# Seven places for gate/up weights in the first quarter of a GEGLU feed-forward, and one low-half computation moved from GpSimd to VectorE

## The chip, the cores and the metric

The kernel runs on one core of a Trainium2 chip. The metric is the device time of one execution in microseconds; three executions are timed and the median counts. One execution is also recorded by the hardware profiler. TensorE does the matmuls, VectorE and ScalarE the elementwise work and the moves out of PSUM, GpSimd some elementwise work on SBUF, and SyncE issues every transfer (DMA) from one queue, in program order.

## The reference

One transformer block with Fourier mixing and a gated feed-forward, for 2048 tokens of 448 features, hidden size 1792, all in float32:

```python
def _A_ref(x, dft_seq_re, dft_seq_im, dft_hid_re, dft_hid_im):
    a = jnp.einsum("bsd,ed->bse", x, dft_hid_re)
    b = jnp.einsum("bsd,ed->bse", x, dft_hid_im)
    return jnp.einsum("ts,bse->bte", dft_seq_re, a) - jnp.einsum("ts,bse->bte", dft_seq_im, b)

def _B_ref(x, w_gate, w_up, w_down):
    g = jnp.einsum("bsd,df->bsf", x, w_gate)
    u = jnp.einsum("bsd,df->bsf", x, w_up)
    return jnp.einsum("bsf,fd->bsd", _gelu(g) * u, w_down)

h = x + _A_ref(_layernorm(x), ...)
h2 = h + _B_ref(_layernorm(h), ...)
```

## The kernel before

**Number format.** Every float32 factor of a matmul is split into two float16 parts, a high half (`hi_part`, line 99, on ScalarE) and a low half (`lo_part`, line 102, on VectorE: the scaled source minus the high half). A product is three matmuls: high by high, high by low, low by high. Sums of blocks (Strassen's scheme) save some of the block products.

**Feature stage.** The tokens form sixteen tiles of 128. Each tile is normalised (`x_stats`, `x_root`, `x_rstd`, `x_norm`), split (`x_high`, `x_lo`), turned so that features lie on the partitions, and multiplied by the feature matrix (`feature_mm`), which gives `a` and `b` side by side. The feature matrix comes in four row blocks k = 0 to 3, block 3 with 64 rows. It is loaded as float32 into `wh_raw` and split into `wh_hi` (`wh_high`) and `wh_lo` (`wh_low`, line 393). `wh_low(k, E)` runs on the engine `E`: on VectorE as one instruction with two SBUF inputs (line 397), on GpSimd as a scaling in place (line 399) and a subtraction (line 400). The work on the first tiles (0, 1, 2, 3, then `a` = 10 and `b` = 11) is written out by hand in lines 705 to 771; each engine runs its share in that order. There, tiles 0 to 3 are turned by TensorE (`x_turn_pe`, PSUM tile `xT_ps`, copied out by ScalarE at line 375). `wh_low(0)`, `(1)` and `(2)` are on VectorE and `wh_low(3, G)` on GpSimd. `feature_mm(i, range(8, 11))` is the part that multiplies by the low halves of blocks 1, 2 and 3; `feature_mm(0, range(8, 11))` follows the turning of tile 3.

**Sequence stage.** From there a planner (`plan`, `todo`) places the work by slots: the remaining tiles, then eight passes over the sequence matrices (`seq_mm`, line 508), eight units each, with VectorE and ScalarE splitting the sequence matrix as it arrives. Meanwhile the gate and up weights are loaded, summed and split (class `Weights`) for each of 14 blocks f of 128 hidden columns. Each block is a float16 tile of 28 x 128 columns and is stored to DRAM (`w_dram[f]`). The order is 13 down to 2, then 0 and 1, so tiles 0, 1 and 2 are still in SBUF when the feed-forward begins; they are `gw[0]`, `gw[1]` and `gw[2]`.

**Feed-forward.** Four quarters q of 512 tokens, 14 blocks f each, are run as 56 iterations t = 14 q + f (the loop at line 1177). In the first quarter an iteration does 39 matmuls of 256 columns (line 913, in `product`) into PSUM banks X, Y and Z. The order on TensorE is:

```python
cur.x_close()
nxt.x_open()
...
cur.y_mid()
nxt.z_open()
nxt.y_open()
cur.y_close()
cur.z_close()
```

`cur` is iteration t, `nxt` is t + 1: the weights of the next iteration are first read in `nxt.x_open()`, early in the present one. `x_open` has ScalarE copy bank X to bank Y (line 952), into which `y_open` goes on adding.

The weight tiles lie in three places in turn: `w_tile` (line 159) takes two from the pool `ring` and one from `ring3`. `gw_load(t)` (line 994) takes the next place and loads `w_dram[t % 14]` into it. Line 1184 calls `gw_load(t + 2)` at the head of iteration t, for t = 1 to 53. The place is that of tile t - 1, so the load may start when the matmuls of iteration t - 1 are done.

Beside this, in the first quarter, the down weights are prepared: `down_prep` loads (`down_load`, line 188, SyncE), sums (`down_sums`, line 192, GpSimd, lines 195 to 198) and splits them (ScalarE and VectorE) over two iterations each. The load for block n + 2 is issued in iteration 2n + 2 behind that iteration's gate/up load; its sums run at the end of iteration 2n + 4.

**Between the stages.** SyncE's queue holds, in this order, the last store of h (`h_store`, line 792), a load of down weights (`down_load(1)`, line 793), then the transfers of the loop. The pool `fpool` of the feed-forward is opened where the sequence stage's pools (`dft`, `p2`) were. Its tag `hh` has two slots, each as large as the hidden state of one quarter (7 x 4 x 256 float32 values for each partition, 28,672 bytes). The quarters 0, 1 and 2 take them in turn (`hh0`, `hh1`, `hh2`), and `h_last` (line 1051) takes one for the last quarter.

Of the kernel before, what the change touches and what calls it, by code (L numbers as in the profile page):

```python
# [8 lines left out]
F16 = mybir.dt.float16  # L9
F32 = mybir.dt.float32  # L10
# [3 lines left out]
P = 128  # L14
S, D, DF = 2048, 448, 1792
NT = S // P
NF = DF // P
# [15 lines left out]
def kernel(  # L33
# [38 lines left out]
    V, A, G, PE = nc.vector, nc.scalar, nc.gpsimd, nc.tensor  # L72
# [3 lines left out]
    small = ctx.enter_context(tc.tile_pool(name="small", bufs=3))  # L76
    ring = ctx.enter_context(tc.tile_pool(name="ring", bufs=2))
# [24 lines left out]
    def lo_part(dst, src, hi, scale=1.0):  # L102
        if isinstance(scale, float) and scale == 1.0:
            V.tensor_sub(dst, src, hi)  # L104
        else:
            V.scalar_tensor_tensor(dst, src, scale, hi, op0=ALU.mult, op1=ALU.subtract)  # L106
# [52 lines left out]
    def w_tile(name, pool):  # L159
        return pool.tile([P, 28 * P], F16, tag="w", bufs=2 if pool is ring else 1, name=name)  # L160
# [6 lines left out]
    def hops_tile(q):  # L167
        hops[q] = ring.tile([P, N_OPS, 2 * P], F16, tag="ops", bufs=2, name=f"hops{q}")
# [12 lines left out]
    def ffn_rstd(q, j):  # L181
        mv, sd = moments[q, j]
        moments[q, j] = mv, rstd(mv, sd, f"h{q}_{j}", const)
# [4 lines left out]
    def down_load(n):  # L188
        wd32[n] = fops.tile([P, 4, HD], F32, tag="tt" if n % 2 else "xn", name=f"wd32_{n}")
        nc.sync.dma_start(wd32[n].rearrange("p (k c) d -> p k (c d)", k=2), w_down[n])  # L190
# [17 lines left out]
    def ffn_norm_act(q, j, h):  # L208

        tag = f"h{q}_{j}"  # L210
        mv, r = moments.pop((q, j))
        xn = fops.tile([P, 2, D], F32, tag="xn", name=f"xn_{tag}")
        nb = small.tile([P, 2], F32, tag="nb", name=f"nb_{tag}")
        V.scalar_tensor_tensor(nb, mv[:, :, 0], -1.0, r, op0=ALU.mult, op1=ALU.mult)
        for g in range(2):
            A.activation(xn[:, g, :], h[:, g, :], AF.Identity, scale=r[:, g : g + 1], bias=nb[:, g : g + 1])
        ffn[q, j] = xn
# [89 lines left out]
    def x_stats(*tiles):  # L307
        n, tag = len(tiles), f"x{tiles[0]}"
        mv = small.tile([P, n, 2], F32, tag=f"mv{n}", name=f"mv_{tag}")
        for g, i in enumerate(tiles):  # L310
            st = small.tile([P, 6], F32, tag="st", name=f"st_x{i}")
            V.bn_stats(st, xt[i][0])
            V.bn_aggr(mv[:, g, :], st)
        norm_x[tiles] = mv
# [4 lines left out]
    def x_rstd(*tiles):  # L319
        mv, sd = norm_x.pop(tiles)  # L320
        r = rstd(mv, sd, f"x{tiles[0]}")
        for g, i in enumerate(tiles):
            norm_x[i] = mv, r, g

    def x_bias(*tiles):
        mv, r, _ = norm_x[tiles[0]]
        nb = small.tile([P, 2], F32, tag="nb", name=f"nb_x{tiles[0]}")
        V.scalar_tensor_tensor(nb, mv[:, :, 0], -1.0, r, op0=ALU.mult, op1=ALU.mult)
        for i in tiles:
            norm_x[i] += (nb,)  # L330

    def x_norm(i):
        x_norm_v(i)
        x_high(i)

    def x_norm_v(i):
        mv, r, g, *nb = norm_x.pop(i)
        xn = xt[i][0]
        if nb:
            A.activation(xn, xn, AF.Identity, scale=r[:, g : g + 1], bias=nb[0][:, g : g + 1])  # L340
        else:
            normed(xn, xn, mv, r, g)
        u, g = divmod(i, 2)
        if g == 0:
            pool = (fops, p1)[ORDER.index(u) % 2]
            t = pool.tile([P, 2, 2 * D], F16, tag="xs", name=f"xs{u}")
            for k in range(2):
                xs[i + k] = t[:, k, :]

    def x_high(i):  # L350
        hi_part(xs[i][:, 0:D], xt[i][0])

    def x_lo(i):
        xn, t = xt[i][0], xs[i]
        lo_part(t[:, D : D + DR], xn[:, DM:D], t[:, DM:D])
        lo_part(t[:, D + DR : 2 * D], xn[:, 0:DM], t[:, 0:DM])
# [12 lines left out]
    def x_turn_pe(i, k0, k1):  # L369
        if k0 == 0:  # L370
            xT_tile(i)
        t = ps_dft.tile([P, 8, P], F16, tag="A", name=f"xT_ps{i}_{k0}")
        for k in range(k0, k1):
            PE.transpose(t[:, k, :], xs[i][:, k * P : (k + 1) * P], ident)
        A.activation(xT[i][:, k0:k1, :], t[:, k0:k1, :], AF.Copy)
# [17 lines left out]
    def wh_low(k, E=V):  # L393
        n = P if k < 3 else DR
        src, hi = wh_raw[k // 2][:n, k % 2, :], wh_hi[:n, k, :]
        if E is V:
            lo_part(wh_lo[:n, k, :], src, hi, D_SC)
        else:
            E.tensor_scalar(src, src, D_SC, None, op0=ALU.mult)
            E.tensor_sub(wh_lo[:n, k, :], src, hi)  # L400
# [218 lines left out]
    def at(t, n, *what):  # L619
        t.setdefault(n, []).extend(what)  # L620
# [112 lines left out]
    feature_mm(0, range(4, 6))  # L733
    x_turn_pe(1, 0, 4)
    x_turn_pe(1, 4, 7)
    wh_low(3, G)
    x_stats(2)
    x_root(2)
    feature_mm(0, range(6, 8))
# [10 lines left out]
    wh_low(2)  # L750
    x_rstd(3)
    x_norm(3)
    x_lo(3)
    a, b = tiles_of[2]
    feature_mm(2, range(7), "A")
# [16 lines left out]
    ring3 = None  # L772
    for n in range(min(todo), len(slots)):
        for _, what in sorted(todo.pop(n, ()), key=lambda t: t[0]):
            what()
        if n == p1_end:
            first.close()
            ring3 = ctx.enter_context(tc.tile_pool(name="ring3", bufs=1))
# [15 lines left out]
    gw = {f: gu[f].w for f in range(3)}  # L794
# [69 lines left out]
    fpool = ctx.enter_context(tc.tile_pool(name="fpool", bufs=1, side="right", reuse_waits="tile"))  # L864
# [63 lines left out]
    hh, hq = {}, {}  # L928

    class GateUp:  # L930
# [58 lines left out]
        def c_last(self):  # L989
            A.activation(self.c12, self.c12, AF.Gelu_apprx_tanh, scale=1.0 / H_SC)  # L990
            c22 = self.hidden(1)
            G.tensor_mul(c22, c22, self.c12)  # L992

    def gw_load(t):
        gw[t] = w_tile(f"gw{t}", ring if t % 3 < 2 else ring3)
        nc.sync.dma_start(gw[t], w_dram[t % NF])


# [36 lines left out]
    def hr_load(p):  # L1035
        hr[p] = pair_tile(f"hr{p}")
        nc.sync.dma_start(hr[p], h_dram[p])
# [12 lines left out]
    def last_begin():  # L1050
        last["h"] = fpool.tile([P, 2, NF, 2 * TQ], F16, tag="hh", bufs=2, name="h_last")
        w = ring.tile([P, N_OPS, 2 * P], F16, tag="ops", bufs=2, name="w_last")
        w = w.rearrange("p o d -> p (o d)")[:, : 4 * NC * HD]
        last["w"] = w.rearrange("p (l n k d) -> p l n k d", l=2, n=NC, k=2)
# [39 lines left out]
    def dn_ahead(t):  # L1094

        if t in (NF - 4, NF - 3):
            dn_sums(t - NF + 4)
        if t == NF - 2:
            dn_split(0)
        if NF <= t < 6 * NC + 12:  # L1100
            dn_sums(t - 12)

    N_GU = 4 * NF
# [4 lines left out]
    def do(t, k):  # L1108
        for what in side.pop((t, k), ()):
            what()  # L1110
# [25 lines left out]
    for t in range(3 * NF, N_GU):  # L1136
        f = t % NF
# [29 lines left out]
    at(side, (25, 4), lambda: ffn_root(NB - 1, 1))  # L1167
    at(side, (27, 1), lambda: ffn_rstd(NB - 1, 1))

    cur = GateUp(0)  # L1170
    cur.x_open()
    cur.z_open()
# [4 lines left out]
    for t in range(N_GU):  # L1177
        q, f = divmod(t, NF)
        if f == 0 and q < 3:
            hh[q] = fpool.tile([P, NC, 4, TQ], F32, tag="hh", bufs=2, name=f"hh{q}")  # L1180
            if 1 <= q <= 2:
                hops_tile(q + 1)
        if 0 < t < N_GU - 2:
            gw_load(t + 2)
        if t == 3 * NF:
            last_begin()
            down_load(0)
            down_load(1)
        if q == 3:
            hq[t] = fpool.tile([P, 2, TQ], F32, tag="hq", bufs=2, name=f"hq{t}")  # L1190
        d = t - NF
        if d >= 0 and d % NC == 1:
            hr_load(d // NC)
        if t in (N_GU - 2, N_GU - 1):
            hr_load(t - N_GU + 8)
        nxt = GateUp(t + 1) if t + 1 < N_GU else None
        if q == 0:
            cur.x_close()
            nxt.x_open()
            if prev:  # L1200
                prev.c_last()
# [5 lines that stand above are left out]
            dn_ahead(t)  # L1207
            if t > 0:
                down_prep(t - 1)
        else:  # L1210
            do(t, 0)
            prev.c_last()
            cur.x_close()
            if t > NF:
                cur.z_open()
            if d + 1 < 6 * NC:
                dn_split(d + 1)
            dn_mm(d, range(0, 8))
            cur.y_mid()
            dn_ahead(t)  # L1220
            dn_mm(d, range(8, 18))
            if nxt:
                nxt.x_open()
            do(t, 1)
            do(t, 4)
            cur.y_close()
            cur.z_close()
            dn_mm(d, range(18, 21))
            do(t, 5)
            if nxt:  # L1230
                nxt.y_open()
            if t == 2 * NC:
                down_hi(NC - 1, 1)
            if t == 2 * NC + 1:
                down_lo(NC - 1, 1)
            do(t, 2)
            do(t, 3)
        prev, cur = cur, nxt
# [72 lines left out]
```

## Time and profile before

| | us |
|---|---|
| median of three runs | 728.72 (728.53 to 728.88) |
| the profiled execution | 728.71 |
| its span, first to last instruction | 726.9 |
| TensorE, matmuls busy | 712.0 (98%) |
| TensorE, weight loads busy | 561.6 (77%) |
| VectorE busy | 510.6 (70%) |
| ScalarE busy | 365.0 (50%) |
| GpSimd busy | 207.9 (29%) |

The transfers moved 142.90 MB, 197 GB/s over the whole span. The mean granted clock of TensorE was 0.998 of full speed. The first gate/up matmul of the feed-forward began at 362.49 us of the span, and the first quarter lasted to about 430 us.

How to read it: "busy" adds up the recorded durations of an engine's instructions. Matmuls overlap in TensorE's pipeline, so a record is longer than the step from one matmul to the next. In a list of waits, each row gives who waited, for whom, the sum in us, how often, and the longest. In a timeline, each row gives start and length in us, engine, line, operation, written tile and read tiles, shapes, count, and in brackets the idle time before it with what ended it.

### The profile page before, as it was taken

To read this page: it belongs to the slowest core of one execution; us is meant where nothing else is said; L and a number is where in the kernel's file an instruction comes from. 1 tells how busy PE (TensorE), PEld (TensorE's weight loads), DVE (VectorE), ACT (ScalarE), POOL (GpSimd) and SP (SyncE) were. 2 spreads that over 40 slices of the span, in tenths; PEclk is the share of its full clock that TensorE was granted. 3 is DMA by queue.
4 is the path that set the end of the run, shared out by engine and by line. 5 is a ranking of instruction groups with operands and counts; after the bars stand their busy time and mean duration, and the time that the engine had idled before them with its cause. 6 is when DMAs were issued, how large, how long until landed. Compare 5 with 4: busy or idle time off the path is not lost.

```text
span 726.9 us, 14535 instructions
## 1 busy us (share of the span) xinstructions
PE 712.0 (98%) x5800; PEld 561.6 (77%) x5800; DVE 510.6 (70%) x1043; ACT 365.0 (50%) x748; POOL 207.9 (29%) x237
## 2 busy tenths in 40 slices
PE   7999999999999999999999999999999999999998
PEld 5556566666767666676788789999999999999998
DVE  6678859998989888989345567576665756667520
ACT  5476644645555545444155555456555545555510
POOL 3023030000000000020014464465563756657230
PEclk9999999999999999999999999999999999999999
DMA  8274444897969699685067754757458486555401
GB/s 326 60 187 93 73 171 148 287 256 259 276 240 282 234 275 326 242 298 187 1 223 240 243 191 169 198 179 223 163 171 205 162 215 223 204 200 203 153 15 64
DMA packets 72340, 142.90 MB, mean 197 GB/s; under 512 B 41296, under 2 KB 47568, under 8 KB 72272
## 3 DMA queue, kind: packets, MB, share of 16 engines
q1 hardware_dynamic: 72272, 141.97, 61.1%
q8 instruction: 45, 0.74, 0.4%
q14 instruction: 23, 0.19, 0.1%
HBM read 112.46 MB, written 20.19 MB: 182 GB/s over the span
## 4 chain that ended last, share of the span: by engine, by line
PE 79%; DVE 10%; DMA 5%; ACT 3%; issue 1%; SPq 0%; DVEq 0%; ACTq 0%
PE acc L508 28%; PE pY L913 13%; PE acc_d L855 11%; PE pZ L913 8%; PE pX L913 8%; PE ab L412 7%; DMA gw<-w_dram 3%; DVE ws L106 2%; DVE xs L104 1%; DMA wr<-in_w_seq_dram 1%; PE last_Z L1079 1%; PE last_X L1079 1%; PE last_Y L1079 1%; DMA gu_raw<-in_w_gu_dram 1%; DVE gu_w L106 1%
## 5 line engine op out<-in xcount | busy, mean ns | idle before, releaser
L508 PE MATMUL acc<-b,ws 128*128 128x448 f16 (+1 forms) x1968 | 280.0, 305 | 1.5 <-DVE ws L106 1.5
L508 PEld LDWEIGHTS <-ws 128*128 128x128 f16 x1968 | 190.0, 98 | 91.1 <-DVE ws L106 3.1
L913 PEld LDWEIGHTS <-gw 128*128 128x128 f16 x2067 | 201.4, 98 | 26.9 <-DMA gw<-w_dram 5.4
L913 PE MATMUL pY<-hops,gw 128*128 128x256 f16 x901 | 122.5, 273 | 0.0
L855 PE MATMUL acc_d<-wd,dn_w 128*128 128x224 f16 x882 | 105.1, 259 | 0.0
L855 PEld LDWEIGHTS <-dn_w 128*128 128x128 f16 x882 | 85.0, 98 | 2.8
L106 DVE SCALAR_TENSOR_TENSOR ws<-wr,ws 128x1024 f16<-128x1024 f32 (+2 forms) x88 | 73.7, 859 | 17.6 <-ACT ws L100 16.4
L100 ACT ACTIVATE ws<-wr 128x1024 f16<-128x1024 f32 (+2 forms) x88 | 64.1, 756 | 41.8 <-issue 26.5
L913 PE MATMUL pX<-hops,gw 128*128 128x256 f16 x583 | 79.7, 273 | 4.5 <-DMA gw<-w_dram 4.5
L913 PE MATMUL pZ<-hops,gw 128*128 128x256 f16 x583 | 80.9, 273 | 0.4 <-DVE hh L923 0.3
L195 POOL TENSOR_TENSOR wd_s<-wd 128x448 f32<-128x448 f32 x7 | 8.2, 1170 | 229.1 <-DMA w_dram<-gu_w 209.8
L992 POOL TENSOR_TENSOR hh<-hh,c 128x256 f32<-128x256 f32 x42 | 31.3, 746 | 145.2 <-ACT c L990 145.2
L412 PEld LDWEIGHTS <-xT 128*128 128x128 f16 x352 | 34.7, 99 | 33.0 <-issue 2.6
L104 DVE TENSOR_TENSOR dn_w<-hh,dn_w 128x256 f16<-128x256 f32 x42 | 19.6, 466 | 53.1 <-ACT dn_w L100 53.1
L1010 POOL TENSOR_TENSOR dn_s<-hh 128x256 f32<-128x256 f32 x42 | 52.8, 1256 | 0.0
L104 DVE TENSOR_TENSOR dn_w<-dn_s,dn_w 128x640 f16<-128x640 f32 x42 | 46.2, 1101 | 6.3 <-ACT dn_w L100 5.2
L957 ACT ACTIVATE u<-pY 128x256 f32<-128x256 f32 x56 | 21.4, 382 | 57.3 <-PE pY L913 57.3
L412 PE MATMUL ab<-wh_hi,xT 128*128 128x448 f16 x224 | 46.7, 359 | 0.2
L952 ACT ACTIVATE pY<-pX 128x256 f32<-128x256 f32 x56 | 20.6, 368 | 51.9 <-PE pX L913 51.7
L1009 POOL TENSOR_TENSOR dn_s<-hh 128x256 f32<-128x256 f32 x42 | 37.9, 902 | 0.0
L971 ACT ACTIVATE u<-pY 128x256 f32<-128x256 f32 x56 | 21.4, 382 | 27.2 <-PE pY L913 26.9
L100 ACT ACTIVATE ws<-wsum 128x1024 f16<-128x1024 f32 x24 | 25.2, 1051 | 18.9 <-DVE wsum L472 18.9
(130 smaller groups left out, 899.5 us busy)
## 6 DMA issues: line engine op xcount, KB each, us to landing
gw<-w_dram SPq DMA_DIRECT2D x53, 896.0 KB, 4.7
wr<-in_w_seq_dram SPq DMA_DIRECT2D x64, 512.0 KB, 4.7
w_dram<-gu_w SPq DMA_DIRECT2D x14, 896.0 KB, 7.2
gu_raw<-in_w_gu_dram SPq DMA_DIRECT2D x28, 384.0 KB, 5.6
wd<-in_w_down_dram SPq DMA_DIRECT2D x14, 448.0 KB, 4.3
hx<-in_x_dram SPq DMA_DIRECT2D x8, 448.0 KB, 6.8
h_dram<-hx SPq DMA_DIRECT2D x8, 448.0 KB, 6.8
hr<-h_dram SPq DMA_DIRECT2D x8, 448.0 KB, 5.4
```

The lines of the kernel that those rows point to most:

```text
L100: A.activation(dst, src, AF.Copy, scale=scale)
L104: V.tensor_sub(dst, src, hi)
L106: V.scalar_tensor_tensor(dst, src, scale, hi, op0=ALU.mult, op1=ALU.subtract)
L412: PE.matmul(feat[i][r][:, :D], xT[i][:, kx, :], w[:, kw, r * D : (r + 1) * D], start=n == 0, stop=n == 10,)
L508: PE.matmul(banks[k][:, cols], lhs, rhs, start=k not in begun, stop=stop, skip_group_check=True)
L855: PE.matmul(acc[k // 2][:, k % 2 * HD : (k % 2 + 1) * HD], a_of(la, a), b_of(lb, b), start=first and m == 0 and k % 2 == 0, stop=last and ...
L913: PE.matmul(ps, w[:, wl, wa + ws, :], ops[:, m + ms, :], start=first and n == 0, stop=last and n == len(terms) - 1, skip_group_check=True,)
L957: A.activation(self.u2, self.Y, AF.Copy, scale=SC)
L992: G.tensor_mul(c22, c22, self.c12)
L1009: G.tensor_add(s[:, 0:2], t[:, 0:2], t[:, 2:4])
L1010: G.tensor_sub(s[:, 2:4], t[:, 1:4:2], t[:, 0:4:2])
L1079: PE.matmul(banks[0][:, c * HD : (c + 1) * HD] if one else banks[c][:, 0:HD], last["h"][:, lh, f, tok], w, start=f == 0 and m == 0 and c = ...
```

## The change

Two edits and a renaming.

1. Before the loop four gate/up tiles, 3 to 6, are loaded into a new tile `ahead` with four places. It takes a slot of the tag `hh`, of the same size. In iterations 1 to 7 the tile six ahead is loaded: 7, 8 and 9 into the places of 0, 1 and 2, and 10 to 13 into the four places again. From iteration 12 on the tile two ahead is loaded, as before. Which of the three old places is `ring3`'s follows `t % 3` in a new way, since now tile 9 is the first to take it again. `hh0` gets the other slot, and `hh1` the one that held `ahead`.
2. `wh_low(3)` runs on VectorE, behind `x_norm(3)`, in place of GpSimd earlier on.
3. The small tile `nb` is named by its size in both functions that use it; both make it two wide, so nothing else differs.

```diff
-        nb = small.tile([P, 2], F32, tag="nb", name=f"nb_{tag}")
+        nb = small.tile([P, 2], F32, tag="nb2", name=f"nb_{tag}")
...
-        nb = small.tile([P, 2], F32, tag="nb", name=f"nb_x{tiles[0]}")
+        nb = small.tile([P, len(tiles)], F32, tag=f"nb{len(tiles)}", name=f"nb_x{tiles[0]}")
...
     x_turn_pe(1, 4, 7)
-    wh_low(3, G)
     x_stats(2)
...
     x_norm(3)
+    wh_low(3)
     x_lo(3)
...
+    ahead = fpool.tile([P, 4, 28 * P], F16, tag="hh", bufs=2, name="gw_ahead")
+
     def gw_load(t):
-        gw[t] = w_tile(f"gw{t}", ring if t % 3 < 2 else ring3)
+        if 3 <= t < 7 or 10 <= t < 14:
+            gw[t] = ahead[:, (t - 3) % 7]
+        else:
+            gw[t] = w_tile(f"gw{t}", ring if t % 3 else ring3)
         nc.sync.dma_start(gw[t], w_dram[t % NF])
...
+    for t in range(3, 7):
+        gw_load(t)
     cur = GateUp(0)
...
-        if 0 < t < N_GU - 2:
+        if 0 < t < 8:
+            gw_load(t + 6)
+        if NF - 2 <= t < N_GU - 2:
             gw_load(t + 2)
```

## The prediction

> **What bounds the kernel now.** I read the page first: its span, and the chain of work that ended last.
>
> ```profile
> span 726.9 us, 14535 instructions
> ...
> PE 79%; DVE 10%; DMA 5%; ACT 3%; issue 1%; SPq 0%; DVEq 0%; ACTq 0%
> ```
>
> TensorE carries four fifths of the chain, so an edit pays only where TensorE stands still or runs slowly. The profiled execution took 728.71 us by its own clock, 1.8 us more than its span, and the median of the three runs is 728.72 us: a microsecond of span is taken as a microsecond of time.
>
> Next, the waits of TensorE, longest first, which say where it stands still.
>
> ```profile
> PE pX L913 <- DMA gw<-w_dram: 4.5, 3, 1.6
> PE xT_ps L374 <- DVE xs L104: 2.3, 3, 1.9
> ...
> PE pZ L913 <- DVE hh L923: 0.3, 1, 0.3
> ```
>
> The reader sees three waits for gate/up weights, 4.5 us in all, and one of 1.9 us for a transpose at the start. The change touches both places. In the whole feed-forward TensorE otherwise waited only 0.3 us, for VectorE: between the three stalls the other engines keep pace with an unbroken TensorE.
>
> Why the weights come late is in the chain in order of time, in the SyncE queue's timeline, and in the list of DMA issues:
>
> ```profile
> 377.70 6.06 DMA gw<-w_dram
> ```
>
> ```profile
> 365.43 0.32 SPq L550 DMA_DIRECT2D h_dram<-hx  x1
> 365.84 0.38 SPq L190 DMA_DIRECT2D wd<-in_w_down_dram  x1
> 369.22 4.59 SPq L996 DMA_DIRECT2D gw<-w_dram  x2
> ```
>
> ```profile
> gw<-w_dram SPq DMA_DIRECT2D x53, 896.0 KB, 4.7
> ...
> wd<-in_w_down_dram SPq DMA_DIRECT2D x14, 448.0 KB, 4.3
> ```
>
> A load may start only when the tile three back has been read, and is needed a little over one iteration later. Normally it lands in 4.7 us; behind a load of down weights, issued by every second iteration, it took 6.06, and TensorE waited.
>
> **Part one, the places for weights.** The number of loads stays 53; no engine instruction is added. Removed: the three stalls. The idle of 4.5 us is counted from the end of the last matmul's record, but the next could have started one step after its start. The step comes from a row of TensorE's timeline and one of the page's groups:
>
> ```profile
> 387.53 1.36 PE L913 MATMUL pX<-hops,gw 128*128 128x256 f16 x11
> ```
>
> ```profile
> L913 PE MATMUL pY<-hops,gw 128*128 128x256 f16 x901 | 122.5, 273 | 0.0
> ```
>
> Eleven matmuls in 1.36 us, and one record of 273 ns by the page's group, so the step is (1.36 - 0.273)/10 = 0.109 us and each stall cost 0.164 us more: 4.5 + 3 x 0.164 = **5.0 us**.
>
> Moved: four loads go to the front, behind the store of h and the down weights at 365.43 and 365.84, and seven (tiles 7 to 13) are issued four iterations earlier, past the down-weight loads in SyncE's queue. Each of the seven still waits for the tile of the iteration just finished, so SyncE stands at the same moments as before, and what is behind it (the next down weights) is issued no later. The four places lie where the Fourier stage's tiles lay. The store of h at 365.43 waits for the last result of that stage and stands ahead of them in SyncE's queue, so they have nothing left to wait for. The same memory later holds a hidden-state buffer, whose first write needs matmuls of the second quarter that follow the last reads of the places on TensorE: no cost.
>
> What is late next is the transfer queue. The rate at which it drains under load is in the table by stage (from left: stretch, length, TensorE, its weight loads, VectorE, ScalarE, GpSimd, granted clock, DMA share, GB/s):
>
> ```profile
> 11.70:14.20 2.50, 2.05 (x10) 0.87 (x9) 2.00 (x9) 0.40 (x2) 2.42 (x2) 1.00 1.01 400
> 18.00:19.00 1.00, 1.00 (x5) 0.45 (x4) 0.97 (x3) 0.80 (x3) 0.00 (x0) 0.50 0.13 49
> 400.90:402.60 1.70, 0.12 (x2) 0.00 (x0) 1.22 (x2) 1.41 (x2) 0.73 (x2) 1.00 0.61 165
> ```
>
> All sixteen engines busy give 400 GB/s. The down weights issued at 365.84 land 4.3 us later, at 370.1. A gate/up tile is 896 KB, 0.918 MB, so 2.3 us at that rate: tile 3 lands about 372.4, before its first use (it was issued at 369.22 and came in time, 4.7 us later). The next down weights stand behind six such tiles (3 to 8): 6 x 2.3 + 1.15 = 15.0 us, landing at 385.1. They are wanted here:
>
> ```profile
> 389.59 1.13 POOL L195 TENSOR_TENSOR wd_s<-wd 128x448 f32<-128x448 f32 x1 [3.43 <-issue]
> ```
>
> That is 388.1 once the first stall (a third of 5.0, here 1.5) is gone: 3.0 us to spare. Behind this GpSimd sum wait ScalarE's casts of its result, and behind them in ScalarE's queue the copy that opens the next product; so any lateness beyond the 3.0 us reaches TensorE in full. The margin is gone when 5.96 MB need 18.0 us, at 331 GB/s. Later loads of this kind gain, since the queue gets less than it drains.
>
> [...]
>
> **Part two, the feature matrix's last low halves.** Two GpSimd instructions go, a scaling and behind it this subtraction:
>
> ```profile
> 14.19 1.89 POOL L400 TENSOR_TENSOR wh_lo<-wh_raw,wh_hi 64x896 f16<-64x896 f32 x1
> ```
>
> GpSimd has nothing else there. One VectorE instruction of the kind in this group (shortest, median, longest ns) comes in its place, after the norm of tile 3:
>
> ```profile
> L106 DVE SCALAR_TENSOR_TENSOR wh_lo<-wh_raw,wh_hi x3: 1059/1084/2755, 10.7 to 18.3; 128x896 f16<-128x896 f32 x3
> ```
>
> I price it at 1.06 us: fewer partitions, the same row length. The longest of the three is the reason for a gain. VectorE's timeline:
>
> ```profile
> 14.28 2.75 DVE L106 SCALAR_TENSOR_TENSOR wh_lo<-wh_raw,wh_hi 128x896 f16<-128x896 f32 x1
> 16.96 0.68 DVE L104 TENSOR_TENSOR xs<-x,xs 128x64 f16<-128x64 f32 x2
> ...
> 21.21 0.69 DVE L104 TENSOR_TENSOR xs<-x,xs 128x64 f16<-128x64 f32 x2 [0.64 <-ACT xs L100]
> ...
> 23.20 0.18 DVE L313 BATCH_NORM_AGGREGATE mv_x<-st_x 128x2 f32<-128x6 f32 x1
> 25.60 1.16 DVE L106 SCALAR_TENSOR_TENSOR b<-ab,b 128x448 f16<-128x448 f32 x2 [2.21 <-ACT b L100]
> ```
>
> It started 0.09 us after GpSimd's subtraction and ended 0.95 us after that one's end (14.19 + 1.89 = 16.08): it stood until GpSimd was through. Without it, 2.75 - 1.06 = 1.69 us go, and tile 2's low parts, for which TensorE waits, come 1.69 earlier.
>
> ```profile
> 12.23 1.67 PE L412 MATMUL ab<-wh_hi,xT 128*128 128x448 f16 x8
> ...
> 17.69 0.50 PE L374 MATMUL xT_ps<-ident,xs 128*128 128x128 f16 x3 [0.20 <-DVE xs L104]
> 17.99 2.45 PE L412 MATMUL ab<-wh_hi,xT 128*128 128x448 f16 x6
> 20.23 0.77 PE L412 MATMUL ab<-wh_lo,xT 128*128 128x448 f16 x2
> 20.84 2.81 PE L412 MATMUL ab<-wh_hi,xT 128*128 128x448 f16 x14
> 23.49 0.55 PE L374 MATMUL xT_ps<-ident,xs 128*128 128x128 f16 x7
> ```
>
> From 20.84 to 23.49 a matmul takes 2.65/14 = 0.189 us; from 17.99 the first six took 2.24/6 = 0.373, twice that, and the table shows the clock at 0.50. After 13.90 (12.23 + 1.67) TensorE had only a few transposes until 17.69: 3.8 us. The stall at 400.90 was 1.70 us nearly empty, and the clock stayed at 1.00. With the change the hole runs from 13.90 to about 16.3, 2.4 us. That size is not in the trace; it is nearer to the 1.70 that kept the clock, and I take full speed. The 22 matmuls from 16.3 then need 4.16 us instead of 5.50, and the transposes of tile 3 start at 20.5, 3.0 earlier.
>
> [...]
>
> VectorE is next. It is 1.69 earlier, loses 1.06 to the new instruction, and regains the 0.64 that it waited before 21.21: the low parts of tile 3 come 1.27 earlier, still before TensorE asks. The moments of the next tiles, done at 23.38, are done at 22.1. ScalarE waits for them with this root:
>
> ```profile
> 24.77 0.30 ACT L121 ACTIVATE sd_x<-mv_x,eps_t 128x2 f32<-128x2 f32 x1
> ```
>
> Behind TensorE it would start at 21.75; behind VectorE at 22.13, so 2.64 earlier than 24.77. The copies that release VectorE at 25.60 are behind that root in ScalarE's queue and move with it. The 2.21 us that VectorE idled there are the cover for the new instruction; without that cover 1.06 of the gain would go. From there the chain in order of time runs through VectorE and ScalarE and then TensorE, and no transfer that started at a fixed time stands on it, so I carry **2.6 us** to the end. Bounds: 1.7 (clock low as before) to 3.0 (VectorE no limit). The renamed small tiles cost nothing: the same instructions.
>
> **Sum.** 728.7 - 5.0 - 2.6 = **721.1 us**.
>
> **Rivals.**
>
> The clock drops all the same: part two is worth 1.7, 722.0 us. For it: the hole still holds little but transposes, and its size is not in the trace.
>
> Down weights late in part: a drain of 300 GB/s (5.96 MB in 19.9 us, 1.9 too late) gives 723.0. Against: the 400 of the row.
>
> Part two is taken back in the long Fourier stage: only the 5.0 remain, 723.7. Against: no transfer there starts by itself.
>
> The four front loads share the engines instead of going in order, so that tile 3 lands with the fourth at 370.1 + 9.2 = 379.3. It was in use at 373.9 at the earliest (369.22 + 4.7): 5.4 lost, 726.5. Against: the first issues of the program, in 0 to 8 us, landed later the later they were issued:
>
> ```profile
> wh_raw<-in_w_hid_dram SPq DMA_DIRECT2D x4, 448.0 KB, 5.5
> x<-in_x_dram SPq DMA_DIRECT2D x3, 448.0 KB, 8.1
> wr<-in_w_seq_dram SPq DMA_DIRECT2D x2, 512.0 KB, 9.0
> ```
>
> The change doesn't do what it says: the places are not free when SyncE comes to them, the stalls stay, and only part two counts: 726.1. Against: the store ahead of them.
>
> Slower than before: queued loads cost as much as single ones, 4.7 us each. The second down weights then land at 370.1 + 6 x 4.7 + 4.3 = 402.6, 14.5 us after 388.1; GpSimd, ScalarE and TensorE stand for it, and the time is 721.1 + 14.5 = 735.6. It decides from 7.6 us of lateness on, at a drain below 5.96 MB/25.6 us = 233 GB/s. For it: a single load shows 0.918 MB/4.7 us = 195 GB/s. Against: the 400 again.
>
> **How the numbers follow.** Forecast 57%, clock 18%, down weights late in part 10%, part two taken back 6%, shared engines 3%, not doing what it says 2%, slower 4%. The range runs from 719.9 (part two at its upper bound 3.0, and 0.8, a tenth of the sum, for terms sized short) to 723.5, which takes in the clock, the partial lateness and most of the fourth case. A measurement of this kernel tells about 0.2%, 1.5 us, from no change. Faster 0.94, same 0.02, slower 0.04.
>
> **What would show it.** Right: no wait for gate/up weights in TensorE's list; that group's median time to landing well above 4.7 us, without harm; the low-half group at 1.06 us throughout; granted clock 1.00 from 16 to 20 us; TensorE's first feed-forward matmul 2.6 us earlier. Wrong: a wait of ScalarE or GpSimd for the down weights near 388, TensorE waiting for tile 3 near 371, or a clock of 0.50 after 16 us.

## The result and the profile after

| | before | after |
|---|---|---|
| median, us | 728.80 (four runs, beside the changed kernel) | 721.23 (720.68 to 722.09, four runs) |
| profiled execution, us | 728.71 | 722.09, the longest of the four |
| its span, us | 726.9 | 720.3 |
| idle of TensorE for gate/up weights, us | 4.5 in all, in three stalls | none |

The ratio of after to before is 0.9883, with a 95% interval from 0.9843 to 0.9922. The forecast was 721.1 us, with a range from 719.9 to 723.5.

First the page of the changed kernel, its span and the chain that ended last, and then the longest waits of TensorE (who waited for whom: sum in us, how often, longest):

```profile
span 720.3 us, 14532 instructions
...
PE 74%; DVE 13%; ACT 6%; DMA 4%; issue 2%; SPq 0%; ACTq 0%; DVEq 0%
```

```profile
PE acc L508 <- DVE ws L106: 2.2, 5, 0.7
PE pw L94 <- POOL eps_t L86: 1.4, 1, 1.4
PE xT_ps L374 <- ACT xs L100: 1.0, 1, 1.0
PE xT_ps L374 <- DVE xs L104: 0.6, 3, 0.2
PE pZ L913 <- DVE hh L923: 0.3, 1, 0.3
```

The reader is to see that the row for `gw` is gone, and that the wait for `xs` at the start has shrunk from 2.3 us to 0.6. The chain has more VectorE than before (13% against 10%).

**The feed-forward.** TensorE's timeline of the changed kernel at the start of the first quarter, and that of the kernel before at the first of its three stalls (start, length, engine, line, tiles, count, idle before):

```profile
360.90 0.82 PE L913 MATMUL pX<-hops,gu_w 128*128 128x256 f16 x6
```

```profile
383.81 0.83 PE L913 MATMUL pX<-hops,gw 128*128 128x256 f16 x6 [1.34 <-DMA gw<-w_dram]
```

The feed-forward begins 1.6 us earlier than before (360.90 against 362.49), and the span ends 6.6 us earlier (720.3 against 726.9). So 5.0 us lie between. Set each matmul of one trace against the same matmul of the other, and call the time by which it begins earlier the lead. In the feed-forward the lead grows in three steps and nowhere else: by 1.50 us at the matmul that began at 383.81 before, and by 1.76 us at each of those that began at 402.61 and 421.42. These are the three stalls. The first step also bears out the way it was counted: 1.34 of idle and 0.16 for the step between matmuls are 1.50.

**The start.** VectorE's timeline of the changed kernel, then ScalarE's and TensorE's:

```profile
14.39 1.08 DVE L106 SCALAR_TENSOR_TENSOR wh_lo<-wh_raw,wh_hi 128x896 f16<-128x896 f32 x1
15.39 0.69 DVE L104 TENSOR_TENSOR xs<-x,xs 128x64 f16<-128x64 f32 x2
...
18.93 1.08 DVE L106 SCALAR_TENSOR_TENSOR wh_lo<-wh_raw,wh_hi 64x896 f16<-64x896 f32 x1
19.93 0.68 DVE L104 TENSOR_TENSOR xs<-x,xs 128x64 f16<-128x64 f32 x2
...
22.88 1.16 DVE L106 SCALAR_TENSOR_TENSOR b<-ab,b 128x448 f16<-128x448 f32 x2 [0.79 <-ACT b L100]
```

```profile
22.12 0.29 ACT L121 ACTIVATE sd_x<-mv_x,eps_t 128x2 f32<-128x2 f32 x1 [0.24 <-DVE mv_x L313]
```

```profile
16.31 1.30 PE L412 MATMUL ab<-wh_hi,xT 128*128 128x448 f16 x6
...
20.48 0.55 PE L374 MATMUL xT_ps<-ident,xs 128*128 128x128 f16 x7
```

The low half of block 1 takes 1.08 us in place of 2.75. The products of tile 2 begin at 16.31 and not at 17.99, and the first six records take 1.30 us in place of 2.45. The transposes of tile 3 begin at 20.48, 3.0 us earlier than before, and the root of the next tiles at 22.12, 2.65 earlier. VectorE's idle ahead of `b` is 0.79 us, where it was 2.21: the cover for the new instruction is mostly used up.

These moments are counted from the span's start, and this execution was already 0.27 us late before the first place that the change touches: VectorE's low half of block 0 began at 10.98, before at 10.71. In `extra1` below, which has the same start, it began at 10.71 as well. There the products of tile 2 begin at 16.05, the transposes of tile 3 at 20.21 and the root at 21.86. So from the same starting point the change is worth 1.94, 3.28 and 2.91 us at these three places.

**The transfers.** The table by stage of the changed kernel (stretch, length, TensorE, its weight loads, VectorE, ScalarE, GpSimd, granted clock, DMA share, GB/s), then SyncE's timeline, the list of DMA issues from 372 to 374 us (KB, us to landing), a row of the page's list of all issues, and GpSimd's timeline:

```profile
366.00:370.00 4.00, 4.00 (x39) 3.60 (x37) 1.28 (x4) 1.84 (x5) 0.53 (x1) 1.00 0.98 350
370.00:375.00 5.00, 5.00 (x48) 4.47 (x47) 2.06 (x5) 3.29 (x8) 0.92 (x2) 1.00 1.01 423
...
385.00:390.00 5.00, 5.00 (x48) 4.48 (x46) 3.25 (x6) 3.03 (x7) 3.53 (x4) 1.00 1.05 407
```

```profile
364.56 0.39 SPq L190 DMA_DIRECT2D wd<-in_w_down_dram  x1
...
372.78 0.33 SPq L190 DMA_DIRECT2D wd<-in_w_down_dram  x1
```

```profile
wd<-in_w_down_dram SPq DMA_DIRECT2D x1, 448.0 KB, 11.3
```

```profile
gw_ahead<-w_dram SPq DMA_DIRECT2D x8, 896.0 KB, 7.4
```

```profile
386.39 1.13 POOL L195 TENSOR_TENSOR wd_s<-wd 128x448 f32<-128x448 f32 x1 [2.84 <-DVE wd L106]
```

The queue is full and drains at 350 GB/s for the first 4 us and above 400 from then on. The down weights issued at 372.78 land 11.3 us later, at 384.1, and are summed at 386.39: 2.3 us to spare. GpSimd waits there for VectorE, not for the transfer.

### The profile page after: what moved, and what is told of

It is laid out like the page before. It is cut to its first block, busy times and chain, and to the rows that moved or that the text cites. A ratio compares the mean times of both kernels' runs of the same rounds, so it can differ in the third digit from the quotient of the medians.

```text
span 720.3 us, 14532 instructions
## 1 busy us (share of the span) xinstructions
PE 710.4 (99%) x5800; PEld 561.5 (78%) x5800; DVE 510.2 (71%) x1044; ACT 364.7 (51%) x748; POOL 202.6 (28%) x235
## 4 chain that ended last, share of the span: by engine, by line
PE 74%; DVE 13%; ACT 6%; DMA 4%; issue 2%; SPq 0%; ACTq 0%; DVEq 0%
PE acc L508 27%; PE pY L913 14%; PE acc_d L855 11%; PE pZ L913 9%; PE pX L913 9%; DVE ws L106 3%; DVE xs L104 2%; ACT b L100 1%; ACT ws L100 1%; PE last_Z L1084 1%; PE last_X L1084 1%; PE last_Y L1084 1%; DVE st_x L312 1%; ACT x L340 1%; DMA gu_raw<-in_w_gu_dram 1%
## 5 line engine op out<-in xcount | busy, mean ns | idle before, releaser
L913 PEld LDWEIGHTS <-gw 128*128 128x128 f16 x1755 | 171.5, 98 | 17.8 <-issue 0.8
L913 PE MATMUL pY<-hops,gw 128*128 128x256 f16 x765 | 105.2, 273 | 0.0
L913 PE MATMUL pZ<-hops,gw 128*128 128x256 f16 x495 | 68.7, 273 | 0.4 <-DVE hh L923 0.3
L913 PE MATMUL pX<-hops,gw 128*128 128x256 f16 x495 | 68.4, 273 | 0.0
```

The source lines that it names most:

```text
L913: PE.matmul(ps, w[:, wl, wa + ws, :], ops[:, m + ms, :], start=first and n == 0, stop=last and n == len(terms) - 1, skip_group_check=True,)
```

## The experiments

Ten runs follow: nine other kernels, and the changed one once more. For each the table gives the ratio to the kernel before, measured beside it, with its 95% interval, and the span of its profiled execution. Where the intervals are too wide for a term of half a microsecond, the reading rests on the trace.

| label | ratio | interval | span, us |
|---|---|---|---|
| places_only | 0.9908 | 0.9877 to 0.9939 | 722.7 |
| low_only | 0.9942 | 0.9901 to 0.9982 | 723.5 |
| no_wd | 0.9952 | 0.9926 to 0.9978 | 724.7 |
| gp_write | 0.9923 | 0.9887 to 0.9959 | 723.7 |
| clock_fill | 0.9961 | 0.9935 to 0.9988 | 727.9 |
| swap | 0.9891 | 0.9852 to 0.9931 | 721.5 |
| no_low3 | 0.9892 | 0.9858 to 0.9926 | 719.8 |
| extra1 | 0.9878 | 0.9833 to 0.9924 | 720.2 |
| extra2 | 0.9938 | 0.9917 to 0.9959 | 726.1 |
| after_again | 0.9879 | 0.9841 to 0.9918 | 719.7 |

### Part one alone

The changed kernel with the low half of block 3 back on GpSimd:

```diff
     x_turn_pe(1, 4, 7)
+    wh_low(3, G)
     x_stats(2)
...
     x_norm(3)
-    wh_low(3)
     x_lo(3)
```

> Only the places for weights; the low half of block 3 stays on GpSimd. If the terms add as predicted: the start as before (VectorE's longest low-half instruction 2.75 us, clock 0.50 near 18 us), no wait of TensorE for gate/up weights, 5.0 us less than before: about 723.7. If the front loads cost something that the start's gain hid in the changed kernel: well above 724.

The group of low halves (shortest, median, longest ns) and the table by stage for 18 to 19 us of this kernel:

```profile
L106 DVE SCALAR_TENSOR_TENSOR wh_lo<-wh_raw,wh_hi x3: 1058/1084/2755, 10.5 to 18.1; 128x896 f16<-128x896 f32 x3
```

```profile
18.00:19.00 1.00, 1.00 (x5) 0.37 (x3) 0.97 (x2) 0.67 (x2) 0.00 (x0) 0.50 0.09 34
```

The start is that of the kernel before, to the long low half and the clock of 0.50. TensorE's list of waits has no row for `gw`, and the lead grows by the same 1.50, 1.76 and 1.75 us in the first quarter. Its span is 4.2 shorter than before and not 5.0, since in the sequence stage this execution had fallen 0.8 us behind the kernel before, though its start is the same. Part one is worth 5.0 us, and it needs nothing of part two.

### Part two alone

The kernel before with the second edit:

```diff
     x_turn_pe(1, 4, 7)
-    wh_low(3, G)
     x_stats(2)
...
     x_norm(3)
+    wh_low(3)
     x_lo(3)
```

> Only the low half moved to VectorE. Predicted: 2.6 us less, 726.1, with the three waits for gate/up weights (4.5 us) as before. In the profile of the changed kernel 1.1 of 2.7 us were lost again in the sequence stage, so up to 727.2 if that is no accident of one execution.

The same group, and TensorE's longest wait for weights:

```profile
L106 DVE SCALAR_TENSOR_TENSOR wh_lo<-wh_raw,wh_hi x4: 1056/1080/1085, 10.9 to 18.9; 128x896 f16<-128x896 f32 x3, 64x896 f16<-64x896 f32 x1
```

```profile
PE pX L913 <- DMA gw<-w_dram: 2.3, 2, 1.5
```

All four low halves take 1.06 to 1.09 us, the transposes of tile 3 start at 20.40, the root at 22.05, and the clock is 1.00: the start of the changed kernel, without the places. After the start the lead is 2.8 us; at the feed-forward 1.4 to 1.5 of it are left. The stalls for `gw` are two here and 2.3 us in all, though nothing in the first quarter differs from the kernel before. Over four profiled executions with the old places they were 4.5, 2.3, 3.2 and 5.6 us. So part one's 5.0 is the price of the stalls in the profiled execution; in another they may cost half of that, or more.

### Why the weights came late

The kernel before, without the loads of down weights in the first quarter from block 2 on, where the sums take the two blocks loaded ahead:

```diff
                 if n + 2 < NC:
-                    down_load(n + 2)
+                    wd32[n + 2] = wd32[n]
```

> Kernel before, with the loads of down weights for blocks 2 to 6 in the first quarter left out (the sums use the two blocks that are there). If the stalls come from gate/up loads that share the engines with down-weight loads: every load lands in about 4.5 us, TensorE waits under 0.5 us, about 5 us less than before. If one iteration is too short for a load anyway: waits of about 4.5 us as before.

TensorE waits for no `gw`, and the lead grows by 1.50, 1.76 and 1.76 us, as with the places. The stalls come from the down weights that stand ahead of a gate/up tile. Four places and no down weights are worth the same. The span is still only 2.2 us shorter, since TensorE was 1.4 us behind the kernel before at 25 us and 2.2 at the feed-forward. The 1.4 are the clock's: the table by stage shows 0.50 for two stretches of 3.41 us, where before it was one. The other 0.8 were lost in the sequence stage.

```profile
16.66:20.07 3.41, 2.62 (x10) 1.31 (x11) 3.30 (x11) 1.27 (x3) 0.00 (x0) 0.50 0.47 177
20.07:23.48 3.41, 3.41 (x11) 1.36 (x9) 2.62 (x7) 0.58 (x1) 0.00 (x0) 0.50 0.00 0
```

### What held VectorE, and the clock

Two kernels take the start apart. In the first GpSimd keeps the scaling, but writes zeros in place of the subtraction. The second is the kernel before with 40 transposes of the identity put into TensorE's hole ahead of the last transpose that waits there for `xs`.

```diff
-            E.tensor_sub(wh_lo[:n, k, :], src, hi)
+            E.memset(wh_lo[:n, k, :], 0.0)
```

```diff
-    x_turn_pe(2, 0, 4)
+    x_turn_pe(2, 0, 3)
+    fill = ps_dft.tile([P, 8, P], F16, tag="A", name="fill")
+    for k in range(40):
+        PE.transpose(fill[:, k % 8, :], ident, ident)
+    x_turn_pe(2, 3, 4)
...
```

The part left out lets `x_turn_pe` fill one PSUM tile in two calls, with one copy by ScalarE behind the second.

> Kernel before, GpSimd's subtraction replaced by a memset of the same rows (low halves of block 3 are zero); its scaling stays. If it is the subtraction's reading that stops VectorE: VectorE's longest low-half instruction about 1.1 us, clock 1.00, tile 3's transposes 3.0 us earlier, 725.7 to 726.8. If any work of GpSimd there slows VectorE: it stays near 2.7 us and the time near 728.7.

> Kernel before, with 40 transposes of the identity put where TensorE waits for tile 2's low parts; GpSimd's two instructions stay, so VectorE still stands (2.75 us). If the halved clock is a term of its own: clock 1.00 from 16 to 20 us, tile 3's transposes about 1.3 us earlier than before, time about 727.4. If the clock has no part in it: the time before, 728.7.

The group of low halves in the first kernel:

```profile
L106 DVE SCALAR_TENSOR_TENSOR wh_lo<-wh_raw,wh_hi x3: 1058/1072/1085, 10.8 to 16.8; 128x896 f16<-128x896 f32 x3
```

An instruction of GpSimd at the same place holds VectorE no longer once it doesn't subtract; the transposes of tile 3 then start at 20.48, as in the changed kernel. GpSimd's timeline there shows that the two did run beside each other:

```profile
14.18 1.08 POOL L400 MEMSET wh_lo<- 64x896 f16 x1
```

VectorE's low half began at 14.40, within this write, and took 1.07 us. What made 2.75 of it before was the subtraction, not that GpSimd was at work. What in the subtraction does it (that it reads SBUF, twice, or that it takes 1.89 us and not 1.08) this run doesn't separate.

The group, TensorE's timeline, its wait for weights and the clock (table by stage) in the second:

```profile
L106 DVE SCALAR_TENSOR_TENSOR wh_lo<-wh_raw,wh_hi x3: 1058/1084/2759, 11.1 to 18.6; 128x896 f16<-128x896 f32 x3
```

```profile
15.54 2.40 PE L755 MATMUL fill<-ident 128*128 128x128 f16 x40
...
18.21 1.30 PE L419 MATMUL ab<-wh_hi,xT 128*128 128x448 f16 x6
...
22.38 0.55 PE L380 MATMUL xT_ps<-ident,xs 128*128 128x128 f16 x7
```

```profile
18.00:19.00 1.00, 0.96 (x8) 0.60 (x9) 0.97 (x3) 0.97 (x3) 0.00 (x0) 1.00 0.19 74
```

```profile
PE pX L924 <- DMA gw<-w_dram: 5.6, 5, 2.0
```

The long low half is still there (2759 ns), the first products begin 0.22 us later than before (18.21 against 17.99), yet the transposes of tile 3 come 1.1 us earlier (22.38 against 23.49). The clock alone is worth 1.3 us; the forecast had 1.34. The span of this execution was 1.0 longer than before all the same, with stalls for weights of 5.6 us in five places; over all its executions the kernel is 0.4% faster, as far as the interval tells. The start's gain has two causes, then: 1.67 from VectorE and 1.3 from the clock. The remaining 0.3 of the 3.28 above belongs to the same two: the norm of tile 2 (line 137) takes 0.51 us without GpSimd's scaling beside it and 0.66 with it, and the last three transposes of tile 2 lead to the first product in 0.17 us at full clock, in 0.30 before.

### Whether VectorE is the limit of the start

Both kernels start from the changed one. The first has VectorE do the low part of tile 2 ahead of the low half of block 1. The second is without the low half of block 3.

```diff
-    wh_low(1)
     x_lo(2)
+    wh_low(1)
```

```diff
-    G.memset(wh_lo[DR:, 3, :], 0.0)
+    G.memset(wh_lo[:, 3, :], 0.0)
...
     x_norm(3)
-    wh_low(3)
     x_lo(3)
```

> Changed kernel with tile 2's low parts ahead of the low half of block 1 on VectorE. If VectorE is what limits the start now: tile 2's last transposes about 1.0 us earlier, the root for tiles 10 and 11 at the same moment, time as the changed kernel. If TensorE limits: 1.0 us less.

> Changed kernel without the low half of block 3 (zeros in its place). Price of the added VectorE instruction: by the prediction's two limits 0.4 us (3.0 less 2.6), seen at the root for tiles 10 and 11. If nothing covers it: 1.06 us.

The root of the next tiles in ScalarE's timeline, first in the swapped kernel, then in the one without the low half:

```profile
23.70 0.29 ACT L121 ACTIVATE sd_x<-mv_x,eps_t 128x2 f32<-128x2 f32 x1 [0.59 <-DVE mv_x L313]
```

```profile
21.84 0.29 ACT L121 ACTIVATE sd_x<-mv_x,eps_t 128x2 f32<-128x2 f32 x1
```

The swapped kernel comes late to the place, since its clock was 0.50 from 8.1 to 11.5 us; so times are counted from the norm of tile 2 (line 137), which began at 14.81 us there and at 13.96 in the changed kernel. From it to the root are 8.89 us, against 8.16. VectorE's timeline of the swapped kernel shows why:

```profile
14.81 0.51 DVE L137 TENSOR_SCALAR x<-x,mv_x,r_x 128x448 f32<-128x448 f32 x1
15.96 0.69 DVE L104 TENSOR_TENSOR xs<-x,xs 128x64 f16<-128x64 f32 x2 [0.64 <-ACT xs L100]
```

The low part of tile 2 comes sooner, but waits 0.64 us for ScalarE's `xs`, and the root is late by about that much. The swap did less than was meant: counted from that norm, the last transposes of tile 2 begin at 1.90 us against 2.18, so 0.3 earlier and not 1.0. Feeding TensorE sooner by these 0.3 gains nothing here; VectorE's own row of work sets the moment. In the other kernel, whose norm of tile 2 began within 0.02 us of the changed one's, the root is 0.28 us earlier. So the added instruction costs 0.28 of its 1.08 us, where the forecast had 0.4; the rest lies in what VectorE would have waited.

### The room in the queue

The changed kernel with one more load of 896 KB behind the four (then with two): the data goes to a place of the down weights that a later load fills, so only the queue differs.

```diff
     for t in range(3, 7):
         gw_load(t)
+    for k in range(1):
+        n = 6 - 2 * k
+        nc.sync.dma_start(wd[:, n - 1 : n + 1].rearrange("p n l o d -> p (n l o d)")[:, 0 : 28 * P], w_dram[k])
```

> Changed kernel with one more 896 KB load, into memory that is written over later, behind the four front loads. In the changed kernel's profile the second load of down weights landed at 384.1 and was used at 386.4: 2.3 us to spare, and one load takes 2.3. If lateness beyond the spare reaches TensorE in full: about 0 to 0.3 us lost. If the spare is larger: nothing.

> The same with two more loads. Spare 2.3 us, delay 4.6: GpSimd's sums start about 2.3 us late, and TensorE waits about 2.2 us in the first quarter, 723.4. If the sums and ScalarE's casts have room of their own: no wait, 721.2.

GpSimd's timeline and TensorE's waits with one more load, and GpSimd's row, TensorE's wait and the table by stage with two:

```profile
385.96 1.13 POOL L195 TENSOR_TENSOR wd_s<-wd 128x448 f32<-128x448 f32 x1 [3.59 <-DMA wd<-in_w_down_dram]
```

```profile
PE pY L913 <- ACT pY L952: 0.9, 1, 0.9
```

```profile
390.35 1.13 POOL L195 TENSOR_TENSOR wd_s<-wd 128x448 f32<-128x448 f32 x1 [6.04 <-DMA wd<-in_w_down_dram]
```

```profile
PE pY L913 <- ACT pY L952: 3.3, 1, 3.3
```

```profile
391.65:395.06 3.41, 0.36 (x4) 0.17 (x2) 0.32 (x1) 1.46 (x3) 2.60 (x3) 1.00 1.03 411
395.06:398.47 3.41, 3.14 (x15) 2.16 (x15) 0.85 (x2) 1.20 (x4) 0.72 (x1) 0.50 0.97 396
```

GpSimd now waits for the transfer, and TensorE for ScalarE behind it. The down weights landed 11.3, 14.2 and 16.7 us after their issue with none, one and two extra loads: 2.9 and 2.5 us for each. Counted from the first feed-forward matmul (at 360.90 in the changed kernel, 359.70 with one and 361.65 with two), GpSimd's sum came 0.8 us later with one and 3.2 later with two than in the changed kernel, and TensorE lost 1.04 and 3.48 there. Two readings follow. The room in the queue is less than one more tile. And what comes late past it does reach TensorE in full, as the forecast had it, and more: with two extra loads the wait of 3.3 us left TensorE nearly idle for a stretch (0.36 us busy of 3.41), and the next 3.41 us ran at a clock of 0.50. In the medians the two loads cost 3.4 us (724.65 against 721.20 for the changed kernel beside them), but the one load 0.1 (721.30): the 1.0 of the single load stands in its trace alone.

### Once more

The changed kernel itself, unchanged:

> The changed kernel once more, beside the next three. 720.7 to 722.1. If the loss of 1.1 us in the sequence stage belongs to the change, it is there again, of the same size; if it is an accident of one execution, it differs.

The span is 719.7 us, and the lead at the first quarter grows by 1.50, 1.76 and 1.76 us again. What differs is the stretch between the start and the feed-forward. In the first profile the lead was 2.71 us at 100 us, lost 0.38 at the `acc` matmul that began at 104.14 before and 0.5 at the one at 253.28, and was 1.6 at the feed-forward. In this one it was 2.76, lost 0.38 at 268.05 and was 2.3 there. Six profiled executions had the new start at full clock: after, after_again, low_only, gp_write, no_low3 and extra1. Their leads at 100 us were 2.7 to 3.0, and ahead of the first stall in the feed-forward 1.7, 2.3, 1.35, 2.3, 2.15 and 2.9. What ended the first loss is in the chain in order of time of the changed kernel's first profile:

```profile
89.08 6.40 DMA w_dram<-gu_w
```

Behind this store of split weights, 6.40 us long, come ScalarE's `b` and VectorE's `ws`, for which TensorE waited at 101.82. In the kernel before ScalarE's `b` stands behind the same store, but there TensorE doesn't wait.

That looks like a price of the lead, but the other runs speak against it. The changed kernel without part two, `places_only`, has no lead at 100 us (0.05), and it waits at the same matmul behind the same store (its chain in order of time):

```profile
91.74 6.27 DMA w_dram<-gu_w
...
104.35 0.74 PE acc L508 x3
```

From 100 us to the feed-forward it loses 0.87 us against the kernel before, and no_wd, which was late already, loses 0.80. The store has no fixed moment either: it was issued at 91.77 before and 2.69 us earlier in the changed kernel. What differs is how long it took. In the eight traces in which it took 6.2 to 6.4 us TensorE lost 0.2 to 0.4 us at this matmul; in the other four (before 6.0, extra2 5.7, after_again 4.8, extra1 4.5) it lost nothing. So these losses come and go from one execution to the next, with a lead and without, and the profiled execution of the kernel before happened to have few of them. Set against places_only at the last matmul before the feed-forward, the same six executions lead by 2.3 to 3.6 us, 2.9 in the mean. Why the store's time varies no run here shows.

## Why the prediction was right

Its two mechanisms held, each by itself, and so did most sizes:

| step | forecast, us | measured, us |
|---|---|---|
| the three stalls | 5.0 | 1.50 + 1.76 + 1.76 = 5.0 |
| VectorE no longer held by GpSimd | 1.69 | 2.75 - 1.08 = 1.67 |
| the clock | 1.34 | 1.3 (clock_fill) |
| transposes of tile 3 | 3.0 earlier, at 20.5 | 20.48; 3.28 earlier from the same starting point (extra1) |
| the next root | 2.64 earlier, at 22.13 | 22.12; 2.91 earlier from the same starting point |
| price of the added instruction | 0.4 | 0.28 (no_low3) |
| lead carried to the feed-forward | 2.6 | 1.6 and 2.3; 1.4 to 2.9 over six executions; 2.3 to 3.6 against places_only |
| room for the down weights | 3.0 | 2.3; 1.8 in after_again |

- **The stalls** went as counted, in every kernel with the places or without the down weights. What the forecast didn't know is that their size differs from one execution to the next (2.3 to 5.6 us with the old places); it took that of the profiled one, which is near the upper end.
- **The hole and the clock.** That the products of tile 2 began at 16.31, where 16.3 was forecast, and the transposes and the root as close to their forecasts, is chance. The gain was 0.3 us larger, as the norm and the slow transposes were not in the sum, and this execution's late start of 0.27 took as much back. The hole lasted 2.14 us (14.17 to 16.31), where 2.4 was forecast. The clock stayed at 1.00 in the six executions named above, so the rival of 722.0 didn't come about in them. It came in another form: in two more, those of extra2 and swap, the clock was at 0.50 from 9.4 to 12.8 and from 8.1 to 11.5 us, ahead of the hole, and the lead at 100 us was 1.2 and 1.1.
- **The carrying to the end** came out below 2.6 against the one profiled execution of the kernel before, as 0.5 to 1.4 us of the lead were lost in five of six executions. But executions without a lead lost 0.8 and 0.9 us in the same stretch, and against places_only the lead is 2.9 us in the mean. So no run shows that the term was too large, nor that a lead is taken back as in the rival of 723.7. The reason given for the term held where it was looked at: the store that stood on the chain moved with the lead.
- **The room in the queue** was over-sized by 0.7 us. Counted from the first feed-forward matmul, the second down weights were to land at 22.6 (385.1 - 362.49) and landed at 23.2 (384.1 - 360.90); they were wanted at 25.5, as forecast (25.6). Of these 0.6 us, 0.3 is the later issue of the first down weights (364.56, or 3.66 us in, against 3.35 before); the 350 GB/s ahead of 370 us is likely the rest. The 400 of the forecast is below the 407 to 423 that follow. The slower rival (735.6), with loads that cost as much as single ones, falls with these rows and with the 2.5 to 2.9 us that one extra load cost.
- **The landing times** rose as forecast, to a median of 7.4 us for the eight loads into the new places (the kernel before: 4.7), without harm.

The profile's own sum is 6.6 us, a microsecond less than forecast; the medians differ by 7.6, as the profiled execution was the longest of its four. That the forecast lies within 0.2 us of the median is partly luck: what the long Fourier stage loses (0.1 to 1.4 us) and the size of the stalls (2.3 to 5.6) vary by more, and so do the medians of the kernel before beside the experiments (729.1 to 730.0, where the forecast started from 728.7).

## What to carry to other kernels

Where a stream of equal loads has a second stream between them, a stall behind the second one can be cured by depth alone, as it was here (5.0 us of stalls, none left with seven places), and the price to work out is the moment at which the second stream's next load is wanted, counted in full tiles ahead of it. A lead won early is hard to follow to the end, since transfers that are merely just in time may or may not hold up the stages between (here the same store took 4.5 to 6.4 us, and TensorE lost nothing or up to 0.4): before a loss there is put down to the change, see whether an execution without the change loses the same. And before a longer instruction is put on the account of its own engine, look at what a neighbour engine does in the same moments (here 2.75 us beside GpSimd's subtraction, 1.08 without).

## What the runs showed of the hardware

**A partly busy stretch can cost the clock.** The clock was at 0.50 for 3.41 us in the kernel before (17.28 to 20.69), in the swapped kernel (8.07 to 11.48) and in extra2 (395.06 to 398.47), and for twice that in no_wd (16.66 to 23.48). The stretches of 3.41 us ahead of the drops were not idle. TensorE was busy for 0.36 us of it in extra2 (above), for 0.43 in the kernel before (from 13.86), and in the swapped kernel, by its table by stage, for 1.70:

```profile
4.66:8.07 3.41, 1.70 (x25) 1.31 (x23) 2.24 (x10) 1.80 (x3) 0.00 (x0) 1.00 0.93 320
8.07:11.48 3.41, 3.17 (x12) 1.32 (x12) 2.62 (x11) 3.16 (x6) 0.00 (x0) 0.50 1.04 398
```

The drops at the start began at five different moments in five executions (8.07 in swap, 9.36 in extra2, 16.66 in no_wd, 17.28 before, 17.37 in places_only). In the traces of the two kernels the records of the clock begin or change at 7.04, 17.28, 20.69 and 727.25 us before, and at 6.53 and 719.91 in the changed kernel: within each trace whole multiples of 3.413 us apart. Laid out in such steps, each trace shows how much work stood ahead of a drop. Three stretches at full clock had TensorE busy for less than 1.8 us: 0.43 at 13.86 and, at the end of each kernel, 0.03 at 723.84 before and 0.72 at 716.50 in the changed one. Behind each of them the clock was at 0.50. The stretches with the next least work, 1.82 us at 399.57 before and 2.02 at 13.36 in the changed kernel, were followed by 1.00. Those 1.82 us lay on both sides of the stall at 400.90.

The two holes differ in this. Wherever a stretch of 3.41 us is laid on the start of the changed kernel (9 to 20 us), TensorE is busy for at least 2.02 us of it; in the kernel before it can be 0.43, and for 93% of the positions that such steps can have it is no more than the 1.70 ahead of the drop in the swapped kernel. The executions bear this out. Their mean granted clock was 0.999 or 1.000 in all eight of the changed kernel, and in 3 of the 46 of the kernel before that ran beside the experiments; one lowering of 3.41 us goes with 0.998 in the profiled execution of the kernel before.

**Transposes of the identity kept the clock.** Forty of them, 2.40 us in all, stood in the hole of clock_fill, and the clock stayed at 1.00, where the kernels with the same start and without them (before, places_only, no_wd) fell to 0.50. The other executions agree with the profiled one: the mean granted clock of clock_fill was 0.999 or 1.000 in eight of ten, against 3 of 46 in the kernel before. And at the start of that program, where TensorE runs nothing but transposes of the identity (37 in 2.86 us from 2.73 on), the step from one to the next falls from 0.11 us to 0.06 at 4.05 us; in the traces of the two kernels it is 0.11 for all fifty.

**GpSimd can hold VectorE.** An instruction of VectorE with two SBUF inputs took 2.75 us beside GpSimd's subtraction and 1.07 beside its write of zeros. One with a single input, the norm of tile 2, took 0.66 us beside GpSimd's scaling in place in gp_write, and 0.51 in the changed kernel, where GpSimd has nothing there (VectorE's timeline of the one, then of the other):

```profile
13.82 0.66 DVE L137 TENSOR_SCALAR x<-x,mv_x,r_x 128x448 f32<-128x448 f32 x1
```

```profile
13.96 0.51 DVE L137 TENSOR_SCALAR x<-x,mv_x,r_x 128x448 f32<-128x448 f32 x1
```
